# Last MLP block in row halves: gate and value products of a chunk formed side by side, an older down product between

## The chip, the core and the metric

The kernel runs on one core of one Trainium2 chip. The metric is device time in microseconds (us), the median of the runs given. Engines are named as the profile names them: PE is TensorE (matrix products), PEld its weight loads, DVE VectorE, ACT ScalarE, POOL GpSimd, SP SyncE, which issues the DMAs.

## The reference

A local attention with pooled keys and values feeds a gated MLP. Cut to what matters:

```python
# q, k, v: (4, 8, 768, 64); block 32, window 16
scores = concat(masked q @ k.T in the window, q @ k_max.T + log 32)   # k_max: maximum over blocks of 32 keys
attn = softmax(scores) @ concat(v, v_mean)
x = attn, tokens by features                   # (3072, 512)
g = x @ w_gate                                 # w_gate, w_val: (512, 1536)
out = (silu(g) * (x @ w_val)) @ w_out          # w_out: (1536, 512)
```

The weights arrive as 64-bit floats. The kernel splits weights and activations into a high and a low part (`wh`, `wl`, `xh`, `xl`, `ah`, `al`) of a 32-bit type that PE streams faster than float32 (called fp32r in the trace), and each product is formed as three: low weight by high activation, high by low, high by high.

## The kernel before

The 3072 tokens are six blocks of 512 (`NBLK`), k = 0 to 5. For each block the attention is computed for four pairs of heads (`u`, 0 to 3), and its result for a pair is one 128-row slice of the transposed x. The MLP goes over twelve chunks of 128 hidden features (`NJ`, j = 0 to 11). For a chunk:

- `m_up` (L532) forms the gate product g: four slices u of the contraction, three terms each, 12 matmuls of a 128x128 weight with 512 moving columns into one PSUM bank. `m_silu` (L548) takes silu of it on ACT (L550).
- `m_up` forms the value product v in the same way, 12 matmuls into another bank. `m_mul` (L553) multiplies on DVE (L555), `m_high` (L557) rounds to the high part `ah` on ACT (through L162), `m_low` (L563) subtracts for the low part `al` on POOL (through L158; on DVE for the last chunk of the last block).
- `m_down` (L582) forms 12 matmuls more (four groups of 128 tokens, three terms) that add to the four accumulators `acc` (L594). After the last chunk they are copied out and stored by SP's DMAs (L608).

PSUM has eight banks in this kernel: two in the pool `psg` (g and v), two in `psy` (attention), four in `psc` (the accumulators). Small tiles `a`, `ah` and `al` have two buffers each.

The order of the work after block 0 is the order in which the code below is written, and every engine keeps to it. The loop at the end of `body` goes through (k, j) for k = 1 to 5: gate product of the chunk, value product of the chunk, down product of the chunk before. Pieces of the attention of the next block are set between them by `do`; they belong to blocks 2 to 5, so nothing of them is left once block 5 begins. The last piece, the output product `xo` of pair 3 of block 5 (`a_out`, L509) and its splitting into `xh` and `xl`, stands just ahead of the first gate product of block 5.

The products of the attention use PE in smaller pieces than 128x128: the scores `sc` (`a_scores`, L384) contract over 64 rows and fill 64 output rows, with the two heads on rows 0 to 63 and 64 to 127, and their results in two banks; `xo` (L509) contracts over 120 rows and fills 64 output rows. The transposes `pp` (L482) use all rows.

Of the kernel before, what the change touches and what calls it, by code (L numbers as in the profile page):

```python
# [10 lines left out]
F32 = mybir.dt.float32  # L11
# [10 lines left out]
P = 128  # L22
NP = H // 2
NB = S // BLK
QT = 64
# [5 lines left out]
NBLK = B * S // TOK  # L31
NJ = DFF // P
# [105 lines left out]
def body(ctx, tc, qP, kP, vT, vP, kq, kF, qF, vE, vR, vO, wgv, wends, wo, cst_in, out):  # L138
    nc = tc.nc
    def after(x, y):  # L140

        tc.add_manual_dep(
            x, y.name, mybir.DependencyInfo(mybir.DependencyClass.NoSync, mybir.DependencyReason.DATA), reason="order"
        )

    pool = lambda n, b, **k: ctx.enter_context(tc.tile_pool(name=n, bufs=b, **k))
    cst = pool("cst", 1)
# [5 lines left out]
    psg = pool("psg", 2, space=bass.MemoryType.PSUM)  # L153
    psy = pool("psy", 2, space=bass.MemoryType.PSUM)
    psc = pool("psc", NTP, space=bass.MemoryType.PSUM)

    def subtract(e, out, a, b):
        (nc.vector if e == "d" else nc.gpsimd).tensor_tensor(out=out, in0=a, in1=b.bitcast(F32), op=ALU.subtract)  # L158

    def copy(e, out, in_):  # L160
        if e == "a":
            nc.scalar.copy(out, in_)  # L162
        else:
            (nc.vector if e == "d" else nc.gpsimd).tensor_copy(out, in_)


    W = {}
# [61 lines left out]
    KT, VT, ksum, vsum, X, U = {}, {}, {}, {}, {}, {}  # L229
# [302 lines left out]
    A, ACC = {}, {}  # L532

    def m_up(k, j, nm, pairs=range(NP)):
# [5 lines left out]
        for u in pairs:  # L540
            xh, xl = X[k, u]
            cs = slice(u * P, (u + 1) * P)
            for n, (w, x) in enumerate(((wl, xh), (wh, xl), (wh, xh))):
                nc.tensor.matmul(  # L544
                    ps, w[:, cs], x, start=u == 0 and n == 0, stop=u == NP - 1 and n == 2
                )

    def m_silu(k, j):  # L548
        a = mlp.tile([P, TOK], F32, tag="a", name=f"a_{k}_{j}")
        nc.scalar.activation(out=a, in_=A.pop(("g", k, j)), func=AF.Silu)  # L550
        A[k, j] = a

    def m_mul(k, j):  # L553
        a, ps = A[k, j], A.pop(("v", k, j))
        nc.vector.tensor_tensor(out=a, in0=ps, in1=a, op=ALU.mult)  # L555

    def m_high(k, j):  # L557
        a = A[k, j]
        ah = mlp.tile([P, TOK], F32R, tag="ah", name=f"ah_{k}_{j}")
        copy(on or "a", ah, a)  # L560
        A[k, j] = (ah, a)

    def m_low(k, j):  # L563
        ah, a = A[k, j]
        al = mlp.tile([P, TOK], F32R, tag="al", name=f"al_{k}_{j}")
        subtract(on or ("d" if (k, j) == (NBLK - 1, NJ - 1) else "p"), al, a, ah)
        A[k, j] = (ah, al)

    def m_up_gate(k, j, *u):
        m_up(k, j, "g", *([u] if u else []))  # L570

    def m_up_val(k, j, *u):
        m_up(k, j, "v", *([u] if u else []))

    def m_gate(k, j):
        m_up_gate(k, j)
        m_silu(k, j)

    def m_val(k, j):
        m_up_val(k, j)  # L580
        m_mul(k, j)
        m_high(k, j)  # L582
        m_low(k, j)

    def m_down(k, j):
        if j == 0:
            ACC[k] = [psc.tile([P, DM], F32, tag="b", name=f"acc{i}_{k}") for i in range(NTP)]
        ah, al = A.pop((k, j))
        wh, wl = W["o", j]
        for i in range(NTP):  # L590
            ts = slice(i * P, (i + 1) * P)
            terms = ((al, wh), (ah, wl), (ah, wh)) if k < NBLK - 1 else ((ah, wh), (ah, wl), (al, wh))
            for n, (a, w) in enumerate(terms):
                nc.tensor.matmul(  # L594
                    ACC[k][i], a[:, ts], w, start=j == 0 and n == 0, stop=j == NJ - 1 and n == 2
                )
            if j == NJ - 1:
                r = k * TOK + i * P
                parts = 2 if k == NBLK - 1 and i == NTP - 1 else 1
                for h in range(parts):  # L600
                    n = DM // parts
                    cs = slice(h * n, (h + 1) * n)
                    if parts == 1:
                        o = mlp.tile([P, n], F32, tag="o", bufs=3, name=f"o_{k}_{i}")
                    else:
                        o = mlp.tile([P, TOK], F32, tag="a", name=f"o_{k}_{i}_{h}")[:, :n]
                    copy("ad"[(i + h) % 2], o, ACC[k][i][:, cs])
                    nc.sync.dma_start(out[r : r + P, cs], o)  # L608
# [12 lines left out]
    def open_pool(name, bufs=1, **kw):  # L621
        stack[name] = tc.tile_pool(name=name, bufs=bufs, **kw)
        return stack[name].__enter__()
# [49 lines left out]
            wts.append(pool("wts3", 1, reuse_waits="tile"))  # L673

    bias_sb, id_sb, mean_sb = {}, None, None
    dec = open_pool("dec", 3, side="right")
    pro = open_pool("pro")
    make_bias()
# [6 lines left out]
    for n in WARM:  # L685
# [10 lines left out]
        "out": a_out, "outp": a_out_pooled, "split": a_split, "rest": a_rest, "w_load": w_load, "w_abs": w_abs, "w_c1": w_range,  # L696
        "w_c2": w_shift, "w_s1": w_top, "w_s2": w_rest, "w_hi": w_hi, "w_lo": w_lo, "gate": m_up_gate,
        "silu": m_silu, "val": m_up_val, "mul": m_mul, "ah": m_high, "al": m_low, "down": m_down,
        "values": a_values, "load_values": a_load_values, "keys": a_keys, "pool_values": a_pool_values,
        "exp": a_exp, "norm": a_norm, "transpose": a_transpose,  # L700
    }
    traced = nc.cur_bb.bb.instructions
# [33 lines left out]
    def do(place):  # L736
        values = None
        for f, *a in sorted(at.pop(place, ()), key=lambda x: x[0] is not a_norm):
            n = len(traced)
            f(*a)  # L740
            if f is a_out:
                values = traced[-1]
            elif f is a_scores and values is not None:
                after(next(x for x in traced[n:] if x.engine == values.engine), values)

    prev = None
    for n, (k, j) in enumerate(seq):
        m_gate(k, j)
        do(3 * n)
        m_val(k, j)  # L750
        do(3 * n + 1)
        if prev:
            m_down(*prev)
        do(3 * n + 2)
        prev = (k, j)
    m_down(*prev)
    assert not at
    for x in traced[n_before:]:
        if x.engine in last:
# [46 lines left out]
```

## Time and profile before

| what | us |
|---|---|
| median of the 2 runs | 694.46 |
| the runs | 694.31 and 694.61 |
| span of the profiled execution, first to last instruction | 693.0 |
| PE busy in it | 686.5 |
| PEld / ACT / DVE / POOL busy in it | 558.0 / 309.4 / 260.7 / 137.5 |
| block 5's MLP, from its first gate product to its last value product | 587.96 to 683.37 |

The time of the profiled execution itself is its span and what lies around it: the runs are 1.3 to 1.6 us longer than the span. PE's busy share says little by itself, as matmuls overlap in the pipeline: a matmul of 512 columns is shown as 0.39 us long while the next begins 0.23 us after it. The distance from start to start is the cost of one. A row of the timeline gives start, duration, engine, line, tiles (out<-in), shape and count; where a count is above 1, the duration runs from the first start to the last end.

### The profile page before, as it was taken

Reading aid. Unit: us, or ns where it says so; the run is one execution under the profiler, and the core shown is the slowest. Engines: PE = TensorE matmul, PEld = TensorE weight load, DVE = VectorE, ACT = ScalarE, POOL = GpSimd, SP = SyncE. Lnnn points to the kernel's source line nnn. Section 1 sums busy time; section 2 is a strip of 40 time slices with the busy share of each in tenths; the row PEclk is TensorE's granted clock in tenths of the full one; section 3 lists DMA queues with packets and bytes.
Section 4 is the critical chain, followed back from the end, with each engine's and each line's share of the span. In section 5 each row is a group of like instructions: output and inputs, shape, how many; then the busy total and the mean of one; then the engine's idle time right before and its main releaser. Section 6 shows DMA issues by size and latency. Waiting matters only on the chain.

```text
span 693.0 us, 11431 instructions
## 1 busy us (share of the span) xinstructions
PE 686.5 (99%) x4556; PEld 558.0 (81%) x4556; DVE 260.7 (38%) x743; ACT 309.4 (45%) x745; POOL 137.5 (20%) x128
## 2 busy tenths in 40 slices
PE   8999999999999999999999999999999999999997
PEld 5688888878888888888888888888888888888886
DVE  6999999934131223232323313223122131100001
ACT  6968998945351542523515424245243242211111
POOL 3110121112221212212212122121121221111110
PEclk9999999999999999999999999999999999999999
DMA  8899275054220222311304222022121000100001
GB/s 333 322 381 330 69 229 160 24 169 130 60 61 1 61 62 83 84 43 43 107 24 145 68 62 62 3 59 62 61 61 52 10 25 0 61 1 0 1 0 61
DMA packets 52966, 61.94 MB, mean 89 GB/s; under 512 B 23184, under 2 KB 40976, under 8 KB 51376
## 3 DMA queue, kind: packets, MB, share of 16 engines
q1 hardware_dynamic: 52912, 61.20, 27.2%
q8 instruction: 36, 0.59, 0.4%
q14 instruction: 18, 0.15, 0.1%
HBM read 54.90 MB, written 6.29 MB: 88 GB/s over the span
## 4 chain that ended last, share of the span: by engine, by line
PE 97%; DVE 2%; DMA 1%; issue 0%; SPq 0%; ACT 0%; DVEq 0%; ACTq 0%
PE g L544 29%; PE acc L594 29%; PE v L544 28%; PE xo L509 4%; PE pp L482 3%; PE sc L384 3%; DMA kq<-in_kF 1%; DVE p L427 1%; PE xo L517 1%; DVE ks L301 0%; PE pv L355 0%; PE pp L618 0%; PE pv L334 0%; DVE m_g L196 0%; SPq L260 0%
## 5 line engine op out<-in xcount | busy, mean ns | idle before, releaser
L594 PE MATMUL acc<-w_o,ah 128*128 128x512 f32 x576 | 178.2, 390 | 0.0
L555 DVE TENSOR_TENSOR a<-v,a 128x512 f32<-128x512 f32 x72 | 49.7, 690 | 295.2 <-PE v L544 267.2
L544 PE MATMUL g<-xh,w_gv 128*128 128x512 f32 x480 | 160.3, 395 | 0.0
L544 PE MATMUL v<-xh,w_gv 128*128 128x512 f32 x480 | 157.9, 390 | 0.0
L158 POOL TENSOR_TENSOR al<-a,ah 128x512 fp32r<-128x512 f32 x63 | 81.9, 1300 | 328.4 <-ACT ah L162 328.4
L594 PEld LDWEIGHTS acc<-w_o,ah 128*128 128x128 f32 x576 | 108.2, 188 | 22.7
L594 PE MATMUL acc<-w_o,al 128*128 128x512 f32 x288 | 114.6, 398 | 0.0
L550 ACT ACTIVATE a<-g 128x512 f32<-128x512 f32 x72 | 43.1, 599 | 155.7 <-PE g L544 154.2
L544 PEld LDWEIGHTS g<-xh,w_gv 128*128 128x128 f32 x480 | 90.1, 188 | 21.5 <-issue 1.9
L544 PEld LDWEIGHTS v<-xh,w_gv 128*128 128x128 f32 x480 | 90.1, 188 | 18.9 <-issue 0.2
L162 ACT CAST ah<-a 128x512 fp32r<-128x512 f32 x71 | 44.0, 621 | 134.8 <-DVE a L555 134.8
L544 PE MATMUL g<-xl,w_gv 128*128 128x512 f32 x240 | 93.6, 390 | 0.0
L544 PE MATMUL v<-xl,w_gv 128*128 128x512 f32 x240 | 93.4, 389 | 0.0
L441 ACT ACTIVATE p<-p,nm 128x120 f32<-128x120 f32 x192 | 73.2, 382 | 6.1 <-DVE nm L427 5.9
L594 PEld LDWEIGHTS acc<-w_o,al 128*128 128x128 f32 x288 | 54.1, 188 | 10.9 <-issue 0.2
L544 PEld LDWEIGHTS v<-xl,w_gv 128*128 128x128 f32 x240 | 45.1, 188 | 9.3
L544 PEld LDWEIGHTS g<-xl,w_gv 128*128 128x128 f32 x240 | 45.1, 188 | 8.8
L467 POOL TENSOR_TENSOR p<-p,ri 128x960 f32<-128x960 f32 x19 | 34.1, 1796 | 71.8 <-DVE ri L459 62.8
L427 DVE CUSTOM_DVE_ANT_0 p<-sc,bias 128x120 f32<-128x120 f32 x160 | 35.9, 276 | 5.1 <-PE sc L384 3.0
L441 ACT ACTIVATION_READ_ACCUMULATOR p<-p,nm 128x1 f32 x192 | 35.8, 187 | 0.0
L162 ACT CAST xh<-xo 128x512 fp32r<-128x512 f32 x23 | 13.4, 586 | 47.0 <-PE xo L509 47.0
L544 PE MATMUL g<-xh,w_g 128*128 128x512 f32 x96 | 32.7, 401 | 0.0
(99 smaller groups left out, 677.6 us busy)
## 6 DMA issues: line engine op xcount, KB each, us to landing
raw_gv<-in_wgv SPq DMA_DIRECT2D x10, 1024.0 KB, 12.1
raw_o<-in_wo SPq DMA_DIRECT2D x12, 512.0 KB, 7.7
out<-o SPq DMA_DIRECT2D x23, 256.0 KB, 2.1
kt<-in_kP SPq DMA_DIRECT2D x12, 384.0 KB, 3.7
vt<-in_vT SPq DMA_DIRECT2D x12, 384.0 KB, 3.3
kw<-in_kP SPq DMA_DIRECT2D x12, 384.0 KB, 4.5
vw<-in_vP SPq DMA_DIRECT2D x12, 384.0 KB, 3.7
kw<-in_kP SPq DMA_DIRECT2D x16, 192.0 KB, 3.6
```

Source lines behind the costliest of these rows:

```text
L158: (nc.vector if e == "d" else nc.gpsimd).tensor_tensor(out=out, in0=a, in1=b.bitcast(F32), op=ALU.subtract)
L162: nc.scalar.copy(out, in_)
L384: nc.tensor.matmul(sc[h][s * QT : (s + 1) * QT, c * KC : (c + 1) * KC], t["q"][hs, qs], t["kw"][hs, i, :], start=True, stop=True,)
L427: nc.vector.tensor_tensor_reduce(out=t["p"][:, i, :], in0=t["sc"][g][:, c * KC : (c + 1) * KC], in1=bias_sb[0 if n == 0 else 2 if n == S / ...
L441: nc.scalar.activation(out=t["p"][:, i, :], in_=t["p"][:, i, :], func=AF.Exp, scale=-1.0, bias=t["nm"][:, i : i + 1], accum_out=t["sm"][:, ...
L467: (nc.vector if on == "d" else nc.gpsimd).tensor_tensor(out=p, in0=p, in1=ri.rearrange("p (n o) -> p n o", o=1).broadcast_to([P, 2 * NTP, ...
L482: nc.tensor.transpose(ps[:KC, c * P : (c + 1) * P], U[k, u]["p"][:, g * NTP + c, :], id_sb)
L509: nc.tensor.matmul(ps[hs, qs], vw, t["pt"][:n, h, qs], start=k not in OWN or i == 0, stop=k not in OWN)
L544: nc.tensor.matmul(ps, w[:, cs], x, start=u == 0 and n == 0, stop=u == NP - 1 and n == 2)
L550: nc.scalar.activation(out=a, in_=A.pop(("g", k, j)), func=AF.Silu)
L555: nc.vector.tensor_tensor(out=a, in0=ps, in1=a, op=ALU.mult)
L594: nc.tensor.matmul(ACC[k][i], a[:, ts], w, start=j == 0 and n == 0, stop=j == NJ - 1 and n == 2)
```

## The change

In block 5 alone, the gate and the value product of a chunk are formed together. Each 128-row matmul becomes two of 64 rows. In the first turn (`turn` 0) gate takes rows 0 to 63 and value rows 64 to 127, alternating matmul by matmul; in the second turn they swap halves. A turn has 24 matmuls. Between the two turns of chunk j stands the down product of chunk j-2 (for chunks 0 and 1 nothing). The second turn must not start before the last two matmuls of the first are complete: a 128x2 memset on POOL waits for those two, and the first two matmuls of the second turn are made to depend on it. The silu, the multiplication and the two splits of the chunk all stand after the second turn. Both products of a chunk take the two banks of one pool, `psg` for even chunks and `psy` for odd ones.

The number of down products is the same. Block 4's last one now stands ahead of block 5's first up product, and the last two of block 5 stand at the end.

```diff
+    def m_up_halves(k, j, turn):
+
+        nms = "gv"
+        if turn == 0:
+            for nm in nms:
+                A[nm, k, j] = (psg, psy)[j % 2].tile([P, 512], F32, tag="b", name=f"{nm}_{k}_{j}")
+        n0 = len(traced)
+        for u in range(NP):
+            xh, xl = X[k, u]
+            cs = slice(u * P, (u + 1) * P)
+            for n in range(3):
+                for s in range(2):
+                    nm = nms[s ^ turn]
+                    wh, wl = W[nm, j]
+                    w, x = ((wl, xh), (wh, xl), (wh, xh))[n]
+                    rows = slice(s * QT, (s + 1) * QT)
+                    nc.tensor.matmul(
+                        A[nm, k, j], w[rows, cs], x[rows],
+                        start=u == 0 and n == 0 and turn == 0, stop=u == NP - 1 and n == 2 and turn == 1,
+                    )
+        made = [x for x in traced[n0:] if x.engine == mybir.EngineType.PE]
+        sync = mybir.DependencyInfo(mybir.DependencyClass.Sync, mybir.DependencyReason.DATA)
+        if turn == 0:
+            n0 = len(traced)
+            nc.gpsimd.memset(mark, 0.0)
+            for y in made[-2:]:
+                tc.add_manual_dep(traced[-1], y.name, sync, reason="halves")
+            halves[k, j] = traced[-1]
+        else:
+            for x in made[:2]:
+                tc.add_manual_dep(x, halves[k, j].name, sync, reason="halves")
...
+    mark = cst.tile([P, 2], F32, name="mark")
...
     for n, (k, j) in enumerate(seq):
-        m_gate(k, j)
-        do(3 * n)
-        m_val(k, j)
-        do(3 * n + 1)
-        if prev:
-            m_down(*prev)
-        do(3 * n + 2)
-        prev = (k, j)
-    m_down(*prev)
+        if k < NBLK - 1:
...
+        else:
+            if j == 0:
+                m_down(*prev)
+            m_up_halves(k, j, 0)
+            if j > 1:
+                m_down(k, j - 2)
+            m_up_halves(k, j, 1)
+            m_silu(k, j)
+            m_mul(k, j)
+            m_high(k, j)
+            m_low(k, j)
+            for x in range(3):
+                do(3 * n + x)
+    m_down(k, NJ - 2)
+    m_down(k, NJ - 1)
```

How PE's order reads at chunk 2 of block 5 before: the end of the gate product, the value product's start. A name carries chunk or slice first and then a buffer number; `g_2` is chunk 2's gate product, `xh_3` slice 3 of the high part of x, and what stands in brackets is the engine whose signal the row waits for.

```order
L544 MATMUL g_2_5570<-xh_3_5460,w_gv_686 128x512
L544 MATMUL g_2_5570<-xl_3_5461,w_gv_686 128x512
L544 MATMUL g_2_5570<-xh_3_5460,w_gv_686 128x512
L544 MATMUL v_2_5585<-xh_0_4811,w_gv_686 128x512 [waits DVE_49]
L544 MATMUL v_2_5585<-xl_0_4812,w_gv_686 128x512
```

And on PE in the changed program where chunk 3's first turn ends, the down product of chunk 1 follows, and the second turn begins (the rows at L564 contract over 64 rows):

```order
L564 MATMUL v_3_5680<-xh_3_5461,w_gv_777 128x512
L628 MATMUL acc_5_5632<-w_o_839,ah_1_5601 128x512 [waits Activation_49]
L628 MATMUL acc_5_5632<-w_o_839,ah_1_5601 128x512
L628 MATMUL acc_5_5632<-w_o_839,al_1_5603 128x512
L628 MATMUL acc_5_5633<-w_o_839,ah_1_5601 128x512 x2
L628 MATMUL acc_5_5633<-w_o_839,al_1_5603 128x512
L628 MATMUL acc_5_5634<-w_o_839,ah_1_5601 128x512 x2
L628 MATMUL acc_5_5634<-w_o_839,al_1_5603 128x512
L628 MATMUL acc_5_5635<-w_o_839,ah_1_5601 128x512 x2
L628 MATMUL acc_5_5635<-w_o_839,al_1_5603 128x512
L564 MATMUL v_3_5680<-xh_0_4812,w_gv_777 128x512 [waits Pool_49]
L564 MATMUL g_3_5679<-xh_0_4812,w_gv_777 128x512
```

The twelve down matmuls now stand between two halves of the same products, and the wait for POOL stands behind them.

PE in the changed program at the second turn of chunk 1, where no down product stands between the turns:

```order
L564 MATMUL g_1_5547<-xh_3_5461,w_gv_523 128x512
L564 MATMUL v_1_5548<-xh_3_5461,w_gv_523 128x512
L564 MATMUL g_2_5605<-xh_0_4812,w_gv_687 128x512 [waits Activation_49]
L564 MATMUL v_1_5548<-xh_0_4812,w_gv_523 128x512 [waits Pool_49]
L564 MATMUL g_1_5547<-xh_0_4812,w_gv_523 128x512
```

The first matmul of chunk 2 has come ahead of the one that waits; the rest of chunk 1's second turn stands behind the wait (at chunk 0 it is the same).

POOL's order at the start of block 5 before, from block 4's last low part on:

```order
L158 TENSOR_TENSOR al_11_5416<-a_11_5398,ah_11_5414 128x512 [waits Activation_49]
L158 TENSOR_TENSOR al_0_5495<-a_0_5477,ah_0_5493 128x512 [waits Activation_49]
L158 TENSOR_TENSOR al_1_5552<-a_1_5534,ah_1_5550 128x512 [waits Activation_49]
L158 TENSOR_TENSOR al_2_5601<-a_2_5583,ah_2_5599 128x512 [waits Activation_49]
L158 TENSOR_TENSOR al_3_5646<-a_3_5628,ah_3_5644 128x512 [waits Activation_49]
```

And in the changed program:

```order
L158 TENSOR_TENSOR al_11_5417<-a_11_5399,ah_11_5415 128x512 [waits Activation_49]
L572 MEMSET mark 128x2 [waits PE_49]
L158 TENSOR_TENSOR al_0_5545<-a_0_5540,ah_0_5543 128x512 [waits Activation_49]
L572 MEMSET mark 128x2 [waits PE_49,Pool_49]
L158 TENSOR_TENSOR al_1_5603<-a_1_5598,ah_1_5601 128x512 [waits Activation_49]
```

Each memset stands behind the low part of the chunk before, so the second turn of a chunk waits for that too.

## Rows read from the trace of the kernel before

**Rows 1.** The page: span, busy time, the chain that ended last by engine and line.

```profile
span 693.0 us, 11431 instructions
PE 686.5 (99%) x4556; PEld 558.0 (81%) x4556; DVE 260.7 (38%) x743; ACT 309.4 (45%) x745; POOL 137.5 (20%) x128
PE 97%; DVE 2%; DMA 1%; issue 0%; SPq 0%; ACT 0%; DVEq 0%; ACTq 0%
```

**Rows 2.** Stretch of block 5: length, PE, PEld, DVE, ACT, POOL busy (count), clock, DMA.

```profile
590.00:689.00 99.00, 99.00 (x437) 81.60 (x435) 11.07 (x16) 16.63 (x28) 14.20 (x11) 1.00 0.03 12
```

**Rows 3.** Groups of PE in 587.9 to 683.6: shape, count | busy us, mean ns.

```profile
L544 PE MATMUL g<-xh,w_gv 128*128 128x512 f32 x80 | 26.3, 389 | 0.0
...
L544 PE MATMUL v<-xl,w_gv 128*128 128x512 f32 x40 | 15.6, 389 | 0.0
...
L544 PE MATMUL v<-xh,w_v 128*128 128x512 f32 x16 | 5.3, 392 | 0.0
...
L544 PE MATMUL v<-xl,w_v 128*128 128x512 f32 x8 | 3.1, 393 | 0.0
```

**Rows 4.** Timeline of one chunk, all engines.

```profile
639.68 0.39 PE L544 MATMUL g<-xh,w_gv 128*128 128x512 f32 x1
639.91 0.39 PE L544 MATMUL v<-xh,w_gv 128*128 128x512 f32 x1
639.91 0.19 PEld L544 LDWEIGHTS v<-xl,w_gv 128*128 128x128 f32 x1
...
640.16 0.60 ACT L550 ACTIVATE a<-g 128x512 f32<-128x512 f32 x1 [4.08 <-PE g L544]
...
642.40 0.39 PE L544 MATMUL v<-xh,w_gv 128*128 128x512 f32 x1
...
642.89 0.69 DVE L555 TENSOR_TENSOR a<-v,a 128x512 f32<-128x512 f32 x1 [7.47 <-PE v L544]
...
643.62 0.62 ACT L162 CAST ah<-a 128x512 fp32r<-128x512 f32 x1 [2.86 <-DVE a L555]
...
644.32 1.29 POOL L158 TENSOR_TENSOR al<-a,ah 128x512 fp32r<-128x512 f32 x1 [6.87 <-ACT ah L162]
```

**Rows 5.** Chain that ended last, pieces from 555 us on: start, us, what, count.

```profile
555.44 0.87 PE pp L482 x8
556.31 2.76 PE acc L594 x12
559.07 1.08 PE xo L509 x32
560.16 0.98 PE sc L384 x32
```

**Rows 6.** Weight loads and matmuls of the scores, whole span, by form.

```profile
L384 PE MATMUL sc<-kw,q 64*64 64x120 f32 x640 | 21.0, 269 | 0.0
L384 PEld LDWEIGHTS sc<-kw,q 64*64 64x64 f32 x640 | 16.4, 132 | 2.6 <-issue 1.2 <-POOL kw L164 0.4
```

**Rows 7.** Timeline round the attention pieces at 558 to 562 us: PE and its loads.

```profile
558.46 0.61 PE L594 MATMUL acc<-w_o,ah 128*128 128x512 f32 x2
...
559.00 1.01 PEld L509 LDWEIGHTS xo<-pt,vw 120*64 120x64 f32 x32 [0.35 <-issue]
559.00 1.15 PE L509 MATMUL xo<-pt,vw 120*64 120x64 f32 x32
560.08 0.82 PEld L384 LDWEIGHTS sc<-kw,q 64*64 64x64 f32 x32
560.09 1.05 PE L384 MATMUL sc<-kw,q 64*64 64x120 f32 x32
...
561.07 0.19 PEld L544 LDWEIGHTS g<-xh,w_gv 128*128 128x128 f32 x1 [0.16 <-issue]
561.07 0.50 PE L544 MATMUL g<-xh,w_gv 128*128 128x512 f32 x1
...
561.40 0.39 PE L544 MATMUL g<-xl,w_gv 128*128 128x512 f32 x1
```

**Rows 8.** A memset of 16 columns on POOL.

```profile
3.23 0.10 POOL L648 MEMSET bias<- 64x16 f32 x1
```

**Rows 9.** POOL ahead of block 5, and PE there.

```profile
584.84 1.29 POOL L158 TENSOR_TENSOR al<-a,ah 128x512 fp32r<-128x512 f32 x1 [7.04 <-ACT ah L162]
...
586.88 1.15 PE L509 MATMUL xo<-pt,vw 120*64 120x64 f32 x32
```

**Rows 10.** The tail: the last chunk's chain of parts.

```profile
683.37 0.39 PE L544 MATMUL v<-xh,w_v 128*128 128x512 f32 x1
...
684.60 0.62 ACT L162 CAST ah<-a 128x512 fp32r<-128x512 f32 x1 [2.94 <-DVE a L555]
...
685.25 0.69 DVE L158 TENSOR_TENSOR al<-a,ah 128x512 fp32r<-128x512 f32 x1 [0.69 <-ACT ah L162]
```

More of the change, by code (lines that the diff above doesn't have):

```diff
@@ L546, in m_up @@
                 )
+    def m_up_halves(k, j, turn):
[28 more added lines that the diff above has]
+                tc.add_manual_dep(x, halves[k, j].name, sync, reason="halves")
+    halves = {}
     def m_silu(k, j):
@@ L747, in body @@
     for n, (k, j) in enumerate(seq):
-        m_gate(k, j)
-        do(3 * n)
-        m_val(k, j)
-        do(3 * n + 1)
-        if prev:
-            m_down(*prev)
-        do(3 * n + 2)
-        prev = (k, j)
-    m_down(*prev)
+        if k < NBLK - 1:
+            m_gate(k, j)
+            do(3 * n)
+            m_val(k, j)
+            do(3 * n + 1)
+            if prev:
+                m_down(*prev)
+            do(3 * n + 2)
+            prev = (k, j)
+        else:
+            if j == 0:
+                m_down(*prev)
+            m_up_halves(k, j, 0)
[10 more added lines that the diff above has]
+    m_down(k, NJ - 1)
     assert not at
```

## The prediction

> **What bounds the kernel now.** I read the page first, then the stretch of block 5, then a timeline of one chunk. The page gives PE 99% busy and a chain of waits that is 97% PE [rows 1]; the other engines lie beside it. In the stretch of block 5 PE is busy for all of its 99.00 us, the granted clock is 1.00 (the 2.4 GHz level) and the DMA share is 0.03, so neither clock nor memory limits it [rows 2]. A busy PE is no proof of a full one, so the number that counts is the distance between starts. In the timeline of a chunk a value matmul starts at 639.91 and the last of the twelve at 642.40: 2.49 us for eleven steps, 0.227 us each [rows 4]. The weight load of the next matmul takes 0.19 us and starts at 639.91, together with the running one, so loads are hidden [rows 4]. 512 columns at one per cycle of 2.4 GHz would take 0.213 us; 0.014 us per matmul is what could still be won here. The part behind a value product runs DVE 0.69, ACT 0.62, POOL 1.29 us [rows 4] and is needed by PE only a product later, so nothing waits.
>
> **Term 1: the halves.** The twelve chunks of block 5 hold 288 gate and value matmuls: 80 + 40 with most weights and 16 + 8 with the first and last chunk's, once for gate and once for value [rows 3]. They become 576 of 64 rows, in 288 pairs. A half matmul still streams 512 columns, so all hangs on whether the two of a pair run side by side. The nearest rows are the scores, which contract over 64 rows with two heads on the two row halves. A transpose of 128 float32 columns takes 0.87 / 8 = 0.109 us [rows 5], or 0.85 ns a column; 120 columns take 0.102 us, and 32 score matmuls one after another would take 3.3 us. They took 0.98 [rows 5], so 3.3 ran at a time. Their 64 output rows explain a factor of two at most (`xo`, which has that alone, took 1.08 us for 32 x 64 x 0.85 ns = 1.74, a factor of 1.6 [rows 5]); the rest comes from the row halves. So I take the pair as side by side, with the step of 0.227 us as now: 0 us. The ends: 0.213 us a pair gives 288 x 0.014 = 4.0 us less; one half after the other gives 0.454 a pair, 288 x 0.227 = 65 us more. The value nearest to a row of the same type and length is 0.227.
>
> The loads double to 576. The scores' loads take 132 ns each [rows 6], and 32 of them lie within 0.82 us [rows 7], five at a time; two loads of 0.19 us under a step of 0.227 then cost nothing. The Trainium skill, "TensorE: Matmul & The Clock Gate", section "LDWEIGHTS (loading the stationary operand)", says that a load's time goes by its columns, not by its rows: a load of 64 rows is as long as one of 128. No row here has a 64-row load of 128 columns. By that rule, if the loads stood in line, a pair would cost twice the load shown, a rival below.
>
> **Term 2: changing between row halves and whole rows.** Around the attention PE changes its shape three times: whole rows to `xo`, `xo` to scores, scores to whole rows. From the accumulator matmul at 558.46 to the second gate matmul at 561.40 pass 2.94 us [rows 7]. The work in it is two accumulator matmuls (0.454), `xo` as 16 steps of 64 columns (0.87), scores as 8 steps of 120 columns (0.82) and one gate matmul (0.227): 2.37 us. The 0.57 us left over are 0.19 for each change. One sees it in the rows: ahead of `xo` the load engine idles 0.35 us, and the first gate matmul is followed by the next after 0.33 instead of 0.227 us [rows 7]. The change adds such a switch on either side of every down product between turns (chunks 2 to 11: 20), one ahead of the first turn and one behind the last: 22 x 0.19 = 4.2 us. Nothing hides it, as PE is the chain. The ends: 0, if row halves alone need no such change (no row shows that case), and 0.25 with a wider load, 5.5 us. I take 4.2, from the row.
>
> **Term 3: the wait between turns.** A second turn waits for the memset on POOL, which stands behind the low part of the chunk before. Everything PE does stands in line behind the waiting matmul. From the start of the last pair of a second turn, the chain is: matmul 0.39, hand-over 0.10 (642.40 + 0.39 to 642.89), silu 0.60, hand-over 0.03 (as 684.60 + 0.62 to 685.25), DVE 0.69, 0.04, ACT 0.62, 0.08, POOL 1.29 [rows 4, 10], memset 0.10 [rows 8] and 0.10 back to PE, my estimate from the longest hand-over: 4.0 us. PE meanwhile has a first turn of 12 steps, 13 x 0.227 = 2.95 us to the next start. Chunk 1 has no down product there and stalls 1.1 us. Chunk 0 waits for its own first turn alone: 0.39 + 0.10 + 0.10 + 0.10 - 0.227 = 0.5 us. The one matmul of the next chunk that comes ahead of the wait shortens neither, as its partner half still has its twelve. From chunk 2 on the down product adds 12 x 0.227 and two switches: PE comes after 6.0 us to a signal given at 4.0, and 2.0 us of cover hide it; without the down product each would cost 1.1 like chunk 1. Sum 1.6 us; the ends are 1.0 (quicker hand-overs) and 3.0 (a slow memset at the two open places).
>
> **Moved work.** Block 4's last down product comes ahead of block 5's first up product. Its low part ends at 584.84 + 1.29 = 586.13, ahead of `xo` at 586.88 [rows 9]: no wait. It gives the splitting of x 2.7 us more cover, and the accumulators are wanted again only at chunk 2, so the copies and SP's stores have more room. At the end the silu now stands behind the last turn. From the last pair's start the high part is ready at 0.39 + 0.10 + 0.60 + 0.03 + 0.69 + 0.04 + 0.62 = 2.5 us and DVE's low part 0.72 us later, at 3.2 [rows 4, 10]. PE begins the last down product at 0.227 + 0.19 + 2.72 = 3.1 with the high part and needs the low part at 3.6: no wait. Both count 0, and DVE, ACT and SP get nothing more to do.
>
> **Sum.** 0 + 4.2 + 1.6 = 5.8 us on the profiled execution: a span of 698.8 instead of 693.0 us. The runs lie 1.3 to 1.6 us above the span; with the median of 694.46 the forecast is 700.3 us, 0.8% more.
>
> **Rivals.** First, halves that win the 0.014 us of a step: while one half changes weights the other streams. For it speaks that the float32 transposes come within 0.002 us of two cycles a column [rows 5], so PE can run without that gap; against it, that the gap stands although the load begins a whole step early [rows 4]. With the switches it gives 694.5 - 4.0 + 5.8 = 696.3 us. The Trainium skill, "TensorE: Matmul & The Clock Gate", section "The mechanism", says that a load overlaps running matmuls only where the row groups differ; this would speak for the halves. The trace does not agree: the 128-row load at 639.91 runs beside a 128-row matmul.
>
> Second, switches that cost nothing, since only the rows are split and the output keeps its 128 rows. Against it speaks that each of the three changes seen had a gap; for it, that all three changed the output rows too. With the step as it is this gives 694.5 + 1.6 = 696.1, with the gain of the first rival 692.1 us.
>
> Third, slower by far: the two halves of a pair run one after the other. Scores stream a column in two cycles, so two row halves together bring one result per output row and cycle, just what a whole matmul brings [rows 4, 5]. The halves here would bring two. If the way into PSUM takes one, a pair costs 0.427 to 0.454 us: 288 x 0.200 to 0.227 = 58 to 65 us, and with the other terms about 758 to 766 us. It decides from a pair of 0.255 us on: 13.9 us (2%, about what a measurement of this kernel can tell from no change) less 5.8, over 288, is 0.028.
>
> Fourth, loads in line: two of 0.19 us a pair, 0.15 more than now, 288 x 0.15 = 44 us, 744 us in all. Against it stand the 32 score loads within 0.82 us [rows 7].
>
> **How the numbers follow.** Forecast 0.53, with a range of its own of 697 to 703 us (switches of 0.06 to 0.25, waits of 1.0 to 3.0). First rival 0.22, second 0.09, third 0.11, fourth 0.05. The range from 691 to 708 us takes in the first three of these five cases and a pair that is slower by up to 0.027 us, and leaves out the last two. Faster by over 2% would need 680.6 us, for which no case gives a reason: 0.01. Slower by over 2% are the last two: 0.16. Within 2%: 0.83.
>
> **What would show it.** In the profile of the changed kernel the two halves of a pair should start within some 0.01 us of each other and the pairs 0.227 us apart; a distance near 0.43 proves the third rival, one of 0.213 the first, one near 0.38 the fourth. At each down product the load engine should idle as it does ahead of `xo`, with about 0.19 us lost on either side. PE should wait for POOL twice, about 0.5 and 1.1 us, and nowhere else. The forecast is wrong if pairs step by more than 0.255 us, if chunks 2 to 11 wait for the memset, or if the time is under 694 us.

## The result, and the profile after

The changed kernel takes 701.42 us (701.38 and 701.46) against 694.46 us: 6.96 us more, a ratio of 1.0099 with a 95% interval of 1.008 to 1.0118. The forecast was 700.3 us, 5.8 more.

The page of the changed kernel, beside [rows 1]:

```profile
span 699.7 us, 12019 instructions
PE 693.0 (99%) x4844; PEld 556.6 (80%) x4844; DVE 260.6 (37%) x743; ACT 309.6 (44%) x745; POOL 137.9 (20%) x140
...
PEclk9999999999999999999999999999999999999999
```

The span has grown by 6.7 us and PE's busy time by 6.5. The busy time of DVE, ACT and POOL has changed by at most 0.4 us, PEld's by 1.4, and the granted clock is at its full level all along (1.00 in the mean). PE is as "busy" as before: the loss sits between starts of matmuls, where busy time does not show it.

The timeline of PE around the second turn of chunk 2 (start, duration, engine, line, tiles, shape, count):

```profile
608.82 0.39 PE L628 MATMUL acc<-w_o,al 128*128 128x512 f32 x1
609.14 0.49 PE L564 MATMUL v<-xh,w_gv 64*128 64x512 f32 x1
609.14 0.49 PE L564 MATMUL g<-xh,w_gv 64*128 64x512 f32 x1
609.48 0.39 PE L564 MATMUL v<-xl,w_gv 64*128 64x512 f32 x1
609.48 0.39 PE L564 MATMUL g<-xl,w_gv 64*128 64x512 f32 x1
609.71 0.39 PE L564 MATMUL v<-xh,w_gv 64*128 64x512 f32 x1
609.72 0.39 PE L564 MATMUL g<-xh,w_gv 64*128 64x512 f32 x1
...
611.79 0.39 PE L564 MATMUL v<-xh,w_gv 64*128 64x512 f32 x1
```

Value and gate start together, so the two halves run side by side. The first pair comes 0.32 us after the last down matmul, the second 0.33 to 0.34 after the first, where [rows 4] had 0.227. The next ten steps, from 609.48 to 611.79, take 0.231 us each in the mean, 0.05 us more in all than ten steps of [rows 4]. The same chunk a little later, with the loads and the other way out:

```profile
612.70 0.39 PE L564 MATMUL g<-xh,w_gv 64*128 64x512 f32 x1
612.70 0.39 PE L564 MATMUL v<-xh,w_gv 64*128 64x512 f32 x1
612.70 0.18 PEld L564 LDWEIGHTS g<-xl,w_gv 64*128 64x128 f32 x1
612.70 0.18 PEld L564 LDWEIGHTS v<-xl,w_gv 64*128 64x128 f32 x1
...
614.51 0.39 PE L564 MATMUL v<-xh,w_gv 64*128 64x512 f32 x1
614.83 0.30 PEld L628 LDWEIGHTS acc<-w_o,ah 128*128 128x128 f32 x2 [0.35 <-issue]
```

From 612.70 to 614.51 there are eight steps of 0.226 us: a pair costs what one whole matmul cost. Both loads of the next pair start with the running one and take 0.18 us each, side by side. Ahead of the down product the load engine idles 0.35 us, just as ahead of `xo` in [rows 7].

PE's waits over the stretch of block 5 (engine, line, whom it waited for, us, times, longest), and POOL's timeline at the second turn of chunk 1:

```profile
PE v L564 <- POOL mark L572: 0.8, 1, 0.8
```

```profile
599.12 1.27 POOL L158 TENSOR_TENSOR al<-a,ah 128x512 fp32r<-128x512 f32 x1 [5.23 <-ACT ah L162]
600.34 0.11 POOL L572 MEMSET mark<- 128x2 f32 x1
```

```profile
599.30 0.39 PE L564 MATMUL v<-xh,w_gv 64*128 64x512 f32 x1
600.49 0.49 PE L564 MATMUL v<-xh,w_gv 64*128 64x512 f32 x1 [0.81 <-POOL mark L572]
```

PE starts a pair at 599.30 and the next at 600.49: 0.97 us more than a step. The step behind it is longer by another 0.11 us, as the next weight load was not ahead. The memset stood behind the low part of chunk 0. At chunk 0 the same place costs 0.40 + 0.11 us:

```profile
593.32 0.39 PE L564 MATMUL g<-xh,w_g 64*128 64x512 f32 x1
...
593.95 0.50 PE L564 MATMUL g<-xh,w_g 64*128 64x512 f32 x1
...
594.29 0.39 PE L564 MATMUL g<-xl,w_g 64*128 64x512 f32 x1
```

The view of waits does not list it, as the pipeline still counts as busy there. From chunk 2 on nothing waits.

### The profile page after: what moved, and what is told of

Its sections match the earlier page's. It is cut to its first block, busy times and chain, and to the rows that moved or that the text cites. A ratio compares the mean times of both kernels' runs of the same rounds, so it can differ in the third digit from the quotient of the medians.

```text
span 699.7 us, 12019 instructions
## 1 busy us (share of the span) xinstructions
PE 693.0 (99%) x4844; PEld 556.6 (80%) x4844; DVE 260.6 (37%) x743; ACT 309.6 (44%) x745; POOL 137.9 (20%) x140
## 4 chain that ended last, share of the span: by engine, by line
PE 97%; DVE 2%; issue 0%; ACT 0%; POOL 0%; ACTq 0%; DVEq 0%
PE acc L628 29%; PE g L544 24%; PE v L544 23%; PE v L564 5%; PE g L564 4%; PE xo L509 4%; PE pp L482 3%; PE sc L384 3%; DVE p L427 1%; PE xo L517 1%; PE warm L652 0%; PE pv L355 0%; DVE ks L301 0%; PE pp L652 0%; PE pv L334 0%
## 5 line engine op out<-in xcount | busy, mean ns | idle before, releaser
L544 PE MATMUL g<-xh,w_gv 128*128 128x512 f32 x400 | 134.0, 396 | 0.0
L544 PE MATMUL v<-xh,w_gv 128*128 128x512 f32 x400 | 131.6, 390 | 0.0
L544 PEld LDWEIGHTS g<-xh,w_gv 128*128 128x128 f32 x400 | 75.1, 188 | 18.4 <-issue 1.9
L544 PEld LDWEIGHTS v<-xh,w_gv 128*128 128x128 f32 x400 | 75.1, 188 | 15.8 <-issue 0.2
L544 PE MATMUL g<-xl,w_gv 128*128 128x512 f32 x200 | 78.0, 390 | 0.0
L544 PE MATMUL v<-xl,w_gv 128*128 128x512 f32 x200 | 77.9, 389 | 0.0
L564 PE MATMUL v<-xh,w_gv 64*128 64x512 f32 x160 | 52.2, 395 | 0.8 <-POOL mark L572 0.8
L564 PE MATMUL g<-xh,w_gv 64*128 64x512 f32 x160 | 52.1, 395 | 0.0
L544 PEld LDWEIGHTS v<-xl,w_gv 128*128 128x128 f32 x200 | 37.5, 188 | 7.7
L544 PEld LDWEIGHTS g<-xl,w_gv 128*128 128x128 f32 x200 | 37.6, 188 | 7.2
```

Of the source, the lines that this page charges most:

```text
L544: nc.tensor.matmul(ps, w[:, cs], x, start=u == 0 and n == 0, stop=u == NP - 1 and n == 2)
L564: nc.tensor.matmul(A[nm, k, j], w[rows, cs], x[rows], start=u == 0 and n == 0 and turn == 0, stop=u == NP - 1 and n == 2 and turn == 1,)
```

## The experiments

A switch is here a change of PE between row halves and whole rows. Theory A: the 6.96 us are switches and two waits, and the pairs cost nothing. The trace gives the price of a switch: from the start of one down product to the start of the next, 606.17 to 614.83, pass 8.65 us, where 36 steps of 0.2267 (those of [rows 4], to one more digit) are 8.16, and two switches lie in between. Half of the 0.49 left over is one switch, 0.245 us. All 22 switches of the changed kernel look alike in the trace: the step across is 0.315 to 0.327 us long and the next one 0.335 to 0.344.

```profile
606.17:614.83 8.65, 8.65 (x61) 6.59 (x61) 0.69 (x1) 1.22 (x2) 1.33 (x3) 1.00 0.01 2
```

This row is the stretch (length, then PE, PEld, DVE, ACT and POOL busy with counts, clock and DMA). There are two rivals. B: the new order of the products costs the time. C: the halves themselves cost it, wherever they stand.

**The order alone (e1_whole_rows).**

```diff
-            m_up_halves(k, j, 0)
+            m_up_gate(k, j)
             if j > 1:
                 m_down(k, j - 2)
-            m_up_halves(k, j, 1)
+            m_up_val(k, j)
```

> Keeps the changed order (both products before the silu, an older down product between them, block 4's last down product first) but forms gate and value product with whole 128-row matmuls, so there is no change between row halves and whole rows and no wait for POOL. Theory A (the 6.96 us are 22 switches and two waits): as before, 694.5 us within 0.4. Rival B (the order costs, since silu, multiplication and splits start later): 696 to 701 us.

Measured: 694.46 us beside 694.5 for the kernel before, ratio 1.0 (0.9992 to 1.0009). PE waits for nothing in block 5. Rival B falls: silu behind both products and the older down product cost nothing.

**Fewer switches (e2_two_chunks).**

```diff
...
-            m_up_halves(k, j, 0)
-            if j > 1:
-                m_down(k, j - 2)
-            m_up_halves(k, j, 1)
-            m_silu(k, j)
+            if j % 2 == 0:
+                for i in (j, j + 1):
+                    m_up_halves(k, i, 0)
+                if j:
+                    for i in (j - 2, j - 1):
+                        m_down(k, i)
+                for i in (j, j + 1):
+                    m_up_halves(k, i, 1)
+                    m_silu(k, i)
...
```

> Halves as in the change, but two chunks share one round trip: first turns of two chunks, down products of the two older chunks, second turns of both. 12 switches instead of 22, and another chunk's first turn covers each signal from POOL. The low part of chunk 10 goes to DVE as chunk 11's does. Theory A: 694.5 + 12 x 0.245 = 697.4 us, no wait for POOL. Rival C (the halves themselves cost, 6.96 us / 288 pairs, wherever they stand): 701.4 us.

Measured: 697.46 us, ratio 1.0041 (1.0028 to 1.0053); no wait for POOL in block 5. That is 2.96 us over 694.5, with 12 switches 0.247 each, as theory A has it. All 288 pairs are still there, so rival C falls.

**No wait (e3_no_wait).**

```diff
             if j == 0:
                 m_down(*prev)
-            m_up_halves(k, j, 0)
-            if j > 1:
+                for i in (0, 1):
+                    m_up_halves(k, i, 0)
+            if j > 1:
+                m_up_halves(k, j, 0)
                 m_down(k, j - 2)
             m_up_halves(k, j, 1)
```

> As the changed kernel, but the first turns of chunks 0 and 1 stand ahead of their second turns, so that neither second turn waits for POOL. Theory A: the two waits (0.51 and 1.07 us with the load that follows) and the slow steps behind them (0.05 each) go: 699.7 us. Rival C: 701.4 us.

Measured: 699.51 us, ratio 1.0076 (1.0063 to 1.0088), without a wait in block 5. The two waits were worth 1.9 us; the trace had given 1.6 and 0.1 of slow steps. The 0.2 us between them lie within the spread of these runs (699.31 to 700.99).

**More switches (e4_split_down).**

```diff
...
-            m_up_halves(k, j, 0)
-            if j > 1:
-                m_down(k, j - 2)
+            if j > 1:
+                for h in (0, 2):
+                    m_up_halves(k, j, 0, range(h, h + 2))
+                    m_down(k, j - 2, range(h, h + 2))
+            else:
+                m_up_halves(k, j, 0)
             m_up_halves(k, j, 1)
```

> As the changed kernel, but each down product of chunks 2 to 11 is cut in two: six matmuls between the two halves of the first turn, six behind it. 20 switches more, nothing else. Theory A with 0.245 us a switch (drain 0.09, load 0.11, slow steps 0.05): 701.4 + 4.9 = 706.3 us; with the 0.19 us of the prediction 705.2 us. Rival C: 701.4 us.

Measured: 705.54 us, ratio 1.0157 (1.0143 to 1.0171): 4.1 us over the changed kernel, 0.206 for each of the 20 switches more, between the two numbers expected. The switches cost by their number, so C falls again, but those in short stretches cost less. PE's timeline there shows the gaps of 0.09 to 0.10 and the late load of 0.11 in full and the steps behind them:

```profile
622.28 0.39 PE L564 MATMUL v<-xh,w_gv 64*128 64x512 f32 x1
622.59 0.73 PE L630 MATMUL acc<-w_o,ah 128*128 128x512 f32 x2
623.16 0.40 PE L630 MATMUL acc<-w_o,al 128*128 128x512 f32 x1
623.39 0.62 PE L630 MATMUL acc<-w_o,ah 128*128 128x512 f32 x2
623.86 0.40 PE L630 MATMUL acc<-w_o,al 128*128 128x512 f32 x1
624.18 0.50 PE L564 MATMUL g<-xh,w_gv 64*128 64x512 f32 x1
...
631.66 0.73 PE L630 MATMUL acc<-w_o,ah 128*128 128x512 f32 x2
```

From 622.59 to 631.66, where the next chunk's first down matmuls start, pass 9.07 us: 36 steps and four switches, where the changed kernel has 8.65 with two. The 0.41 more is 0.207 for each of the two, as in the runs' times.

Behind a gap of the changed kernel ten steps take 0.231 us in the mean instead of 0.2267, 0.05 us together. Here only some four slow steps follow the late load: six matmuls between two gaps leave no room for ten, and behind the last gap of a chunk, where there would be room, the steps are back at 0.227 after four. What these slow steps are stays open; the next run asks what brings them.

**A wait without a switch (e6_wait_only).** The kernel before, whole rows and its own order, with a signal through POOL between gate and value product:

```diff
...
+        m0 = len(traced)
         m_gate(k, j)
...
+            made = [x for x in traced[m0:] if x.engine == mybir.EngineType.PE]
...
+            nc.gpsimd.memset(mark, 0.0)
+            signal = traced[m1]
+            tc.add_manual_dep(signal, made[-1].name, sync, reason="gap")
+        m0 = len(traced)
         m_val(k, j)
...
+            first = next(x for x in traced[m0:] if x.engine == mybir.EngineType.PE)
+            tc.add_manual_dep(first, signal.name, sync, reason="gap")
```

> The kernel before with whole rows and its own order, and a wait for a memset on POOL between gate and value product of each chunk of block 5: twelve gaps without any change of shape. Theory A (a gap costs its length, the next weight load of 0.11 that was not ahead, and slow steps of 0.05 behind it, whatever made the gap): the signal comes 0.63 us after the last gate matmul, one down matmul fills 0.23 of it; 12 x (0.63 - 0.45 + 0.11 + 0.05) = 4.1 us, 698.5 us. Rival D (slow steps only follow a change between halves and whole rows): 12 x 0.29 = 3.5 us, 697.9 us, and steps of 0.227 us at once behind each gap.

Measured: 699.01 us beside 694.6, ratio 1.0066 (1.0053 to 1.0078); 4.4 us for twelve gaps, nearer to theory A's 4.1 than to D's 3.5. The time alone decides little, as the gaps came out longer than either had reckoned: in the trace they take 2.8 us beyond a step (0.21 each as a rule, 0.50 once), the late loads behind them 1.3 and the slow steps 0.3. The timeline of one gap:

```profile
626.44 0.39 PE L544 MATMUL g<-xh,w_gv 128*128 128x512 f32 x1
626.67 0.39 PE L594 MATMUL acc<-w_o,ah 128*128 128x512 f32 x1
627.11 0.50 PE L544 MATMUL v<-xh,w_gv 128*128 128x512 f32 x1
627.45 0.39 PE L544 MATMUL v<-xl,w_gv 128*128 128x512 f32 x1
627.68 0.62 PE L544 MATMUL v<-xh,w_gv 128*128 128x512 f32 x2
628.14 0.40 PE L544 MATMUL v<-xl,w_gv 128*128 128x512 f32 x1
...
628.83 0.39 PE L544 MATMUL v<-xl,w_gv 128*128 128x512 f32 x1
```

The step behind the gap is 0.34 us, as behind a switch. So the late load goes with a gap of PE, not with the change of shape. The next six steps, to 628.83, take 1.38 us instead of 1.36, and then the steps are back at 0.227. So D falls in part: slow steps follow a gap without a switch too, but here they come to 0.02 us, about half of what follows a switch of the changed kernel. The 0.09 us of standing still are the switch's own.

**Which halves meet (e5_same_half).**

```diff
-            for n in range(3):
-                for s in range(2):
+            for s in range(2):
+                for n in range(3):
                     nm = nms[s ^ turn]
...
```

> As the changed kernel, but within a slice the three terms of one half stand together: three gate matmuls on one row half, then three value matmuls on the other, so that only one neighbour in three is on the other half. Theory A with side by side by neighbours only: runs of three take three steps and overlap at their ends, some 109 steps of 0.227 us more, 726 us. If PE looked further ahead and ran any two halves beside each other: 701.4 us. If halves never ran side by side, the changed kernel itself would have shown it: 766 us.

Measured: 701.32 us, ratio 1.0094 (1.0079 to 1.011): the same as the changed kernel. My expectation for theory A, side by side by neighbours only, was wrong by 25 us. PE's timeline where a second turn begins, of a program whose order there is three value, three gate, three value, and then in the first turn of the next chunk, where gate comes first:

```profile
608.90 0.39 PE L628 MATMUL acc<-w_o,al 128*128 128x512 f32 x1
609.22 0.49 PE L564 MATMUL v<-xh,w_gv 64*128 64x512 f32 x1
609.23 0.49 PE L564 MATMUL g<-xh,w_gv 64*128 64x512 f32 x1
...
613.46 0.39 PE L564 MATMUL g<-xh,w_gv 64*128 64x512 f32 x1
613.47 0.39 PE L564 MATMUL v<-xh,w_gv 64*128 64x512 f32 x1
613.68 0.39 PE L564 MATMUL g<-xl,w_gv 64*128 64x512 f32 x1
613.69 0.39 PE L564 MATMUL v<-xl,w_gv 64*128 64x512 f32 x1
```

They run in pairs. At 609.23 the first gate matmul, the fourth of the turn, starts 0.01 us behind the first value matmul: ahead of its place in the program, past two that have not started. How far ahead a matmul can come was open.

**Halves further apart (e7_twelve_apart, e8_six_apart).** In e7 the half is the outermost loop of a turn; e8 does the same for two slices at a time (a step of 2 in the place of 4). In e5, e7 and e8 the signal through POOL waits for the last matmul of each half, and the first of each half waits for it.

```diff
-        for u in range(NP):
...
+        for first in range(0, NP, 4):
+            for s in range(2):
...
+                for u in range(first, first + 4):
...
```

> As the changed kernel, but a turn is written as twelve matmuls on rows 0 to 63 and then twelve on rows 64 to 127, so that the two that ran side by side stand twelve matmuls apart. Theory E (each row half takes its matmuls from the queue by itself, as e5 with three in a row at 701.3 us suggests, however far apart): 701.4 us and starts of gate and value in pairs. Rival F (it looks a few instructions ahead only): a turn takes up to 23 steps instead of 12, up to 24 x 11 x 0.227 = 60 us more, 761 us; anything between tells how far it looks.

> The same with six matmuls in a row on each half. Theory E: 701.4 us. Rival F with a reach under six: runs of six overlap at their ends only, about 21 of 24 steps a turn, 9 x 24 x 0.227 = 49 us more, 750 us; a reach of six or more: 701 to 703 us here and more in the run with twelve.

Measured: 738.64 us (ratio 1.0637, 1.0621 to 1.0653) and 709.3 us (1.0215, 1.0198 to 1.0232). Theory E falls: there is a limit, as rival F had it. F's numbers (up to 761 us, and 750 for a reach under six) were too high, since it took the two halves to overlap at the ends of their rows only. The timelines show more. With twelve in a row, a second turn begins with value at 627.75, and gate's first matmul, the thirteenth of the turn, starts with the ninth value matmul:

```profile
627.43 0.39 PE L628 MATMUL acc<-w_o,al 128*128 128x512 f32 x1
627.75 0.49 PE L564 MATMUL v<-xh,w_gv 64*128 64x512 f32 x1
...
629.48 0.39 PE L564 MATMUL v<-xl,w_gv 64*128 64x512 f32 x1
629.71 0.39 PE L564 MATMUL v<-xh,w_gv 64*128 64x512 f32 x1
629.72 0.49 PE L564 MATMUL g<-xh,w_gv 64*128 64x512 f32 x1
```

With six in a row gate's first, the seventh, starts with the third:

```profile
619.84 0.39 PE L628 MATMUL acc<-w_o,al 128*128 128x512 f32 x1
620.16 0.49 PE L564 MATMUL v<-xh,w_gv 64*128 64x512 f32 x1
620.49 0.39 PE L564 MATMUL v<-xl,w_gv 64*128 64x512 f32 x1
620.73 0.39 PE L564 MATMUL v<-xh,w_gv 64*128 64x512 f32 x1
620.73 0.49 PE L564 MATMUL g<-xh,w_gv 64*128 64x512 f32 x1
```

In both it starts with the matmul four places before its own, past three that have not started. From there on the two halves run side by side. Three in a row lie within that reach, which fits e5's losing nothing.

No run came out faster than the kernel before, and none points to one that would: the best version with halves, e2, still pays for its switches and gets nothing for the pairs.

## Why the prediction was right

**Term 1, the halves: 0 us, right.** Pairs step by 0.226 to 0.227 us like whole matmuls, and the loads lie beside each other. The first rival (0.213 a pair) is out: nothing of the 0.014 us between a step and 512 columns is won by loading one half while the other streams. The third is out: a pair started together takes one step, so two row halves do deliver two results per output row in the time of one, which the scores could not show. The fourth is out by the two loads at 612.70. The Trainium skill, "TensorE: Matmul & The Clock Gate", section "LDWEIGHTS (loading the stationary operand)", says that the time of a load does not go by its rows. The trace agrees: after a gap the late load costs 0.11 us with 64 rows (609.14 to 609.48, less a step) and 0.11 with 128 (at 614.83, in the same way). But that did not put two loads in line.

**Term 2, the switches: right in kind, 4.2 us forecast, 22 x 0.245 = 5.4 measured.** This is the term that was too small. A switch is 0.09 us of standing still, 0.11 for the load that was not ahead, and 0.05 of slow steps. The prediction took 0.19 from [rows 7], where two of the three changes were followed by loads of 64 columns. (Its sum has `xo` a little short: in the trace its products start in pairs 0.058 us apart, not the 0.054 of 64 columns at 0.85 ns, so that 0.17 is left for a change.) With the wider load, standing still and load make 0.20 here. The prediction's upper end of 0.25 is the price measured, but not for the reason given there: the wider load alone stops at 0.20, and the rest is slow steps, which the forecast did not have. That this end held is luck. The slow steps could have been read before the change, behind the first gate matmuls of [rows 7]:

```profile
562.79 0.39 PE L544 MATMUL g<-xl,w_gv 128*128 128x512 f32 x1
```

From 561.40 to here are six steps of 0.232 us. The second rival, switches that cost nothing, is out: row halves with a full 128 output rows cost no less than the attention's shapes. e2 and e4 price them by number.

**Term 3, the waits: right in kind, and in size with some luck.** Forecast 0.5 and 1.1 us, in the trace 0.51 and 1.08 with the late load; taken away, 1.9 us came back (e3). The forecast had no late load in it: the waits alone are 0.40 and 0.97 us, each a little shorter than forecast, and the load of 0.11 makes up for it. Chunks 2 to 11 were covered by the down product, as forecast.

**Moved work: 0 us, right.** e1 has the whole order of the change and the time of the kernel before.

The sum from the trace is 0 + 5.4 + 1.6 = 7.0 us, and 6.96 were measured. The forecast of 5.8 is 1.2 us short, and term 2 is where they are missing.

## What to carry to other kernels

Row halves can help where the contraction is short, as with the scores [rows 5]. Cutting a full 128-row matmul into two that run side by side costs the same step and needs twice the instructions, so there is nothing to win by it on an engine that is the bound. Price a change of shape on PE by its gap, the next load and the steps behind it (0.245 us here, 0.207 for each one added in e4), count the changes, and put the work of one shape together before anything else. A signal through another engine costs what is queued ahead of it there: look at that queue, not at the memset.

## What the runs showed that was not expected

- Matmuls on different row halves do not keep the program's order. The kernel before was described with every engine keeping the written order; here a matmul on the other half started with the one up to four places before it (e7, e8), so pairs need not be neighbours: three in a row cost 701.32 us against 701.42.
- After a gap of PE some steps take 0.231 instead of 0.2267 us: ten behind a switch of the changed kernel, four in e4's short stretches, and five in e6, where the shape does not change. Why, and what sets their number, is open.
